# Logits of blocks 1, 4 and 5 from three bfloat16 pieces of h, four chunks at a time in four column ranges of TensorE's array

## The chip, the cores and the metric

The kernel runs on one core of one Trainium2 chip. The metric is the device time of one execution, in microseconds. Engines are called as the profile calls them: PE is TensorE's matrix multiply, PEld its weight load, DVE is VectorE, ACT ScalarE, POOL GpSimd, SP the engine that issues most DMAs.

## The reference, cut to what matters

Attention with random features gives x (2304 tokens by 512). A gated layer turns x into h (2304 by 1536) and y = h @ w_out. A gate then gives each token eight logits, and a greedy assignment over all logits sorts the tokens to eight experts, each a two-layer network.

```python
xn = x / rms * rms_g
g = xn @ w_gate
silu = g * (1.0 / (1.0 + np.exp(-g)))
val = xn @ w_val
y = silu * val @ w_out              # h = silu * val
logits = y @ moe2_w_gate            # 2304 x 8
order = np.argsort(-logits.flatten())   # greedy: token to expert, at most 288 each
```

The order of the logits decides where a token goes, so they are computed to nearly full float32. The kernel takes them from h with the product w_out @ moe2_w_gate (1536 by 8), made beforehand, so that they need not wait for y.

## The kernel before, in words

Tokens are cut into five blocks j = 0 to 4, four of 512 tokens and a last one of 256 (the title counts them from 1). The 1536 columns of h are cut into twelve chunks f of 128. One step (j, f, v) is twelve matmuls in `ffn_pe` (L659, L660, L662) into one of two PSUM buffers `gv`: v = 0 is the gate, v = 1 the value. After v = 0, ACT takes a tanh into `th` (L671) and DVE multiplies it in (L672); after v = 1, DVE makes the chunk of h (L684). ACT and POOL then split it into a high and a low part in `hp` (L686, L687), both of type float32r, and SP stores them to `h_dr` in DRAM, from where the later product with w_out reads them.

The logits of a chunk are two matmuls (`ffn_lg`, L698 and L699), with the chunk's 128 by 16 gate weights `wog` (a high and a low part for eight experts) as stationary operand and `hp`'s high and low part as moving operand, 512 or 256 columns wide. They stand in the step (j, f+1, 1), one chunk late, and sum over the twelve chunks in the PSUM tile `lg` (`late` for block 0). After chunk 11 ACT copies the 16 by 512 sums out (L702); in the next step `ffn_rank` transposes them in pieces of 16 by 128 (L710), ACT copies half of the result (L712), DVE adds the halves (L713), and `ranks` (L97 to L101) orders each token's eight logits.

Steps of blocks 0 to 2 and the first of block 3 run among the attention's work. Block 0's logits can't be done there, as `wog` is not ready: its h is stored unsplit. What is left then runs in a loop (L905 on): the rest of block 3, then block 4, and beside them block 0 "late": `late_load` (L891) fetches a chunk of block 0 from `h_dr` into a buffer `ht`, `late_split` (L897) splits it on ACT (L899) and POOL (L900) and stores it back, and `ffn_lg` takes its logits a step later. `wo_split` (ACT L876, DVE L877) prepares w_out, through staging buffers `ws`. In this loop Tile's scheduler orders the engines by priority; ahead of it PE's order is as written.

After the loop come six matmuls of y, the last chunk's logits (L1001), block 4's ranks, and `route`, the greedy assignment: a chain of small DVE operations and matmuls, with the product y = h @ w_out (`py`, L972, 648 matmuls of 512 columns) as filler on PE, in an order written by hand (`FILL`). `route` first clears two work areas on POOL (L122), one of them `ge6`.

Of the kernel before, what the change touches and what calls it, by code (L numbers as in the profile page):

```python
# [9 lines left out]
F32 = mybir.dt.float32  # L10
F32R = mybir.dt.float32r
BF = mybir.dt.bfloat16
I32 = mybir.dt.int32
AF = mybir.ActivationFunctionType
OP = mybir.AluOpType
AX = mybir.AxisListType
# [28 lines left out]
DW = 3  # L45
# [8 lines left out]
AHEAD_F = 150  # L54
HB = 6
LATE = 2

C_ID, C_SL, C_SA, C_C, C_P, C_E, C_T, C_N = 0, 128, 224, 248, 266, 267, 275, 339

# [44 lines left out]
def route(nc, keep, sb, ps, cst, L, R, ids, slot, aside, room):  # L104
# [10 lines left out]
    for n in (NSL, SL, 2 * NSL):  # L115
# [1 line left out]
        off += NC * n  # L117
    oa, ob, rt = parts
    ges = {5: room[:, off:off + (NC - 1) * 31 + 128],
           6: sb.tile([128, (NC - 1) * 63 + 128], BF, name="ge6", bufs=1)}  # L120
    for g in ges.values():
        nc.gpsimd.memset(g, 0.0)  # L122
    rt = rt.rearrange("p c (a n) -> p c a n", a=2)
# [168 lines left out]
def kernel(ctx, tc, qT, kT, kC, v1, vC, om, wgv, rms, wo, woT, wg2, w1, w2, cfd, trd, cid, out, dbg=None):  # L292
# [356 lines left out]


    fq, fst, lgs, rks = [], {}, [], []

    def ffn_pe(j, f, v):
        n = WIDTH[j]
# [10 lines left out]
    def ffn_el(j, f, v, pg):  # L665
        n = WIDTH[j]
        nh = n // HB2
        if v == 0:
            fst["th"] = fp.tile([128, BLK], F32, name="th")
            th = fst["th"][:, :n]  # L670
            nc.scalar.activation(th, pg, AF.Tanh, scale=0.5)  # L671
            nc.vector.scalar_tensor_tensor(th, th, 1.0, pg, op0=OP.add, op1=OP.mult)  # L672
            return
        th = fst["th"][:, :n]
        hp = fp.tile([128, BLK // HB2, 2, HB2], F32R, name="hp")
        hf = hp.bitcast(F32)
        dst = h_dr[nh * j:nh * j + nh] if nh > 1 else h_dr[NT // HB2 - 1:]
        dst = dst[:, :, f].rearrange("b p x -> p b x")
        if j == 0:
            nc.vector.scalar_tensor_tensor(hf[:, :, 0], pg.rearrange("p (b t) -> p b t", b=nh), 0.5,  # L680
                                           th.rearrange("p (b t) -> p b t", b=nh), op0=OP.mult, op1=OP.mult)
            nc.sync.dma_start(dst[:, :, :HB2], hf[:, :, 0])
            return
        nc.vector.scalar_tensor_tensor(th, pg, 0.5, th, op0=OP.mult, op1=OP.mult)  # L684
        h = th.rearrange("p (b t) -> p b t", b=nh)
        nc.scalar.copy(hp[:, :nh, 0], h)  # L686
        nc.gpsimd.tensor_sub(hp[:, :nh, 1], h, hp[:, :nh, 0])  # L687
        nc.sync.dma_start(dst, hf[:, :nh].rearrange("p b l t -> p b (l t)"))
        fq.append((j, f, hp))

    def ffn_lg(j, f, hp):
        n = WIDTH[j]
        nh = n // HB2
        if f == 0:
            st["lg", j] = (psL if j else psB).tile([2 * E, BLK], F32, name="lg" if j else "late", bufs=1)
        wv = wog[:, f].rearrange("p a e -> p (a e)")
        lg = st["lg", j][:, :n].rearrange("p (b t) -> p b t", b=nh)
        nc.tensor.matmul(lg, wv, hp[:, :nh, 0], start=(f == 0), stop=False)  # L698
        nc.tensor.matmul(lg, wv, hp[:, :nh, 1], start=False, stop=(f == KF - 1))  # L699
        if f == KF - 1:  # L700
            ls = fp.tile([2 * E, BLK], F32, name="th")
            nc.scalar.copy(ls[:, :n], st.pop(("lg", j))[:, :n])  # L702
            lgs.append((j, ls))

    def ffn_rank():
        for j, ls in lgs:
            n, c = WIDTH[j] // 128, j * BLK // 128
            pl = st["rank"]()
            for i in range(n):
                nc.tensor.transpose(pl[:, i, :], ls[:, i * 128:(i + 1) * 128], ident[:2 * E, :2 * E])  # L710
            lt = fp.tile([128, BLK // 128, E], F32, name="lt")
            nc.scalar.copy(lt[:, :n], pl[:, :n, E:])  # L712
            nc.vector.tensor_add(L[:, c:c + n, :], pl[:, :n, :E], lt[:, :n])  # L713
            rks.extend(range(c, c + n, 2))
        lgs.clear()

    st["eng"] = nc.gpsimd
    st["rank"] = lambda: psL.tile([128, BLK // 128, 2 * E], F32, name="lg")
# [6 lines left out]
    def ffn_step_pe():  # L725
        if not ready or ready[0][1:] not in gvs or (fq and fq[0][1] not in wogs):
            return False
        j, f, v = ready.pop(0)
        pg = ffn_pe(j, f, v)
        if (f, v) == (KF - 1, 1):  # L730
            del xblk[j]
        ffn_rank()
        if v and fq:
            ffn_lg(*fq.pop(0))
        fst["el"] = (j, f, v, pg)
        return True

    def ffn_step_el():
        if "el" in fst:
            j, f, v, pg = fst.pop("el")  # L740
            with tc.high_priority(offset=AHEAD_F):
                ffn_el(j, f, v, pg)
            ffn_rank_el()
            return j, f, v
        return None
# [96 lines left out]
    with tc.manual_schedule(engines={mybir.EngineType.PE}):  # L842
# [13 lines left out]
    rp = fc.enter_context(tc.tile_pool(name="rp", bufs=2))  # L856
    psB = fc.enter_context(tc.tile_pool(name="psB", bufs=2, space=PSUM))
    st["eng"] = nc.vector
    st["rank"] = lambda: psB.tile([128, 512], F32, name="num", bufs=1)[:, :BLK // 128 * 2 * E].rearrange(
        "p (c e) -> p c e", e=2 * E)  # L860
    ci = rp.tile([128, cid.shape[1]], I32, name="ci", bufs=1)
    ones = rp.tile([128, 128], BF, name="ones", bufs=1)
    pw = {sh: rp.tile([128, 128], BF, name=f"pw{sh}", bufs=1) for sh in SHIFTS}
# [7 lines left out]
    def wo_split(c):  # L871
        sv = stage.tile([128, 2, DM], F32, name="ws")
        nc.sync.dma_start(sv, wo_dr[2 * c:2 * c + 2].rearrange("f p d -> p f d"))
        w = wpool.tile([128, 2, 1024], F32R, name="wc")
        sv = sv.rearrange("p f d -> p (f d)")
        nc.scalar.copy(w[:, 0], sv)  # L876
        nc.vector.tensor_sub(w[:, 1], sv, w[:, 0])  # L877
        wos.append(w)
# [7 lines left out]

    order = [*range(BLK // 128, NC - TAIL), *range(BLK // 128), *range(NC - TAIL, NC)]
    seq2 = [(c, g) for c in order for g in range(3)]
    lates, step = [], 0

    def late_load(f):  # L891
        hs = f2.tile([128, 4, 2, 128], F32R, name="ht", bufs=HB)
        hs = hs.rearrange("p a l t -> p (a l t)").rearrange("p (b l t) -> p b l t", b=BLK // HB2, l=2)
        nc.sync.dma_start(hs.bitcast(F32)[:, :, 1], h_dr[:BLK // HB2, :, f, :HB2].rearrange("b p x -> p b x"))
        lates.append(hs)

    def late_split(f):  # L897
        hs = lates[f]
        nc.scalar.copy(hs[:, :, 0], hs.bitcast(F32)[:, :, 1])  # L899
        nc.gpsimd.tensor_sub(hs[:, :, 1], hs.bitcast(F32)[:, :, 1], hs[:, :, 0])  # L900
        nc.sync.dma_start(h_dr[:BLK // HB2, :, f].rearrange("b p x -> p b x"),
                          hs.bitcast(F32).rearrange("p b l t -> p b (l t)"))

    late_load(0)
    while True:  # L905
        if not ffn_step_pe():
            break
        lf, lv = divmod(step, 2)
        if not lv and 0 < lf <= KF:
            ffn_lg(0, lf - 1, lates[lf - 1])  # L910
        j, f, v = ffn_step_el()
        if lv and lf < KF:
            late_split(lf)
            if lf + 1 < KF:
                late_load(lf + 1)
        if j == NB - 1 and v:
            if f % 2 and f > 1:
                wo_split((f - 3) // 2)
            if f > 6:
                ffn2_load(*seq2[f - 7])  # L920
        step += 1
    assert step > 2 * KF
    wo_split(KF // 2 - 1)

    wch = {}
# [72 lines left out]
        return True  # L998

    fill(3 * FILL_MM)  # L1000
    ffn_lg(*fq.pop(0))  # L1001
    fill(3 * FILL_MM)
    ffn_rank()
    ffn_rank_el()
# [213 lines left out]
```

## Time and profile before

| | us |
|---|---|
| median of three runs | 923.66 (919.81 to 926.49) |
| the profiled execution | 922.03 |
| its span, first to last instruction | 920.2 |
| PE busy | 901.9 (98% of the span) |
| PEld busy | 783.3 |
| DVE busy | 554.2 (60%) |
| ACT busy | 372.8 |
| POOL busy | 229.8 |

The span is from the first to the last instruction; the profiled execution's own time holds 1.8 us more. Matmuls are pipelined, so a busy PE is not a PE at its peak: what a matmul costs is read from the distance of two starts, not from its duration.

### The profile page before, as it was taken

How to read it: one execution, taken by the hardware profiler on the slowest of the kernel's cores; microseconds unless marked ns; L12 is line 12 of the kernel's file. 1: busy time of each engine (PE TensorE's matmuls, PEld its weight loads, DVE VectorE, ACT ScalarE, POOL GpSimd, SP SyncE). 2: the span in 40 equal slices, each digit the busy share in tenths (PEclk: the TensorE clock that was granted, in tenths of full speed). 3: DMA queues.
4: the chain of work that ended last, by engine and by line, in shares of the span. 5: the costliest groups of instructions: out<-in, count | busy, mean ns of one | idle time of the engine just before them, and what ended most of it. 6: DMA issues, size and time to landing. Idle time of an engine off the chain costs nothing.

```text
span 920.2 us, 16173 instructions
## 1 busy us (share of the span) xinstructions
PE 901.9 (98%) x6171; PEld 783.3 (85%) x6171; DVE 554.2 (60%) x1262; ACT 372.8 (41%) x843; POOL 229.8 (25%) x298
## 2 busy tenths in 40 slices
PE   8998999999999999999999999999999999999996
PEld 7887888888888888877799777777779999999995
DVE  4798896565676775332273666666654655556661
ACT  5985565435554445333252001000014454544541
POOL 1355352122233332275232000000012222122111
PEclk9999999999999999999999999999999999999998
DMA  8556354444345552187564776776623666665550
GB/s 295 182 160 213 120 168 127 135 152 144 115 153 178 184 185 90 69 278 277 189 225 152 202 207 191 211 206 201 171 78 115 193 188 193 189 208 193 184 161 26
DMA packets 113213, 158.88 MB, mean 173 GB/s; under 512 B 6640, under 2 KB 70768, under 8 KB 113136
## 3 DMA queue, kind: packets, MB, share of 16 engines
q1 hardware_dynamic: 107328, 143.57, 49.4%
q0 software_dynamic: 3072, 9.44, 3.4%
q10 hardware_dynamic: 2736, 4.85, 1.4%
q8 instruction: 48, 0.79, 0.3%
q14 instruction: 29, 0.24, 0.1%
HBM read 113.79 MB, written 44.04 MB: 172 GB/s over the span
## 4 chain that ended last, share of the span: by engine, by line
PE 84%; issue 7%; DVE 5%; POOL 2%; DMA 2%; ACT 1%; SPq 0%; POOLq 0%; ACTq 0%; DVEq 0%
PE py L972 16%; PE gv L659 10%; PE gv L660 10%; PE gv L662 10%; PE pm L497 3%; PE ph L1086 3%; PE ph L1083 3%; PE ph L1084 3%; PE py L1094 3%; PE py L1095 3%; PE py L1096 3%; PE pm L440 2%; PE cnt L181 2%; PE pm L486 2%; PE pp L388 1%
## 5 line engine op out<-in xcount | busy, mean ns | idle before, releaser
L659 PE MATMUL gv<-xh,wc 128*128 128x512 f32 (+1 forms) x480 | 180.9, 383 | 2.5 <-DVE th L672 1.9
L660 PE MATMUL gv<-xh,wc 128*128 128x512 f32 (+1 forms) x480 | 175.3, 372 | 0.0
L972 PE MATMUL py<-wc,ht 128*128 128x512 f32 x648 | 167.1, 404 | 0.0
L972 PEld LDWEIGHTS py<-wc,ht 128*128 128x128 f32 x648 | 114.9, 189 | 19.0
L662 PE MATMUL gv<-xl,wc 128*128 128x512 f32 (+1 forms) x480 | 118.4, 369 | 0.0
L659 PEld LDWEIGHTS gv<-xh,wc 128*128 128x128 f32 x480 | 91.1, 190 | 19.5 <-DVE th L672 3.0
L660 PEld LDWEIGHTS gv<-xh,wc 128*128 128x128 f32 x480 | 91.2, 190 | 13.9
L662 PEld LDWEIGHTS gv<-xl,wc 128*128 128x128 f32 x480 | 85.5, 189 | 15.9
L400 ACT ACTIVATE ft<-pp,mx 128x128 f32<-128x128 f32 x288 | 82.3, 372 | 18.5 <-DVE mx L397 16.0
L687 POOL TENSOR_TENSOR hp<-th,hp 128x512 fp32r<-128x512 f32 (+1 forms) x48 | 60.6, 1262 | 114.5 <-ACT hp L686 102.6
L672 DVE SCALAR_TENSOR_TENSOR th<-th,gv 128x512 f32<-128x512 f32 (+1 forms) x60 | 37.9, 632 | 84.4 <-ACT th L671 84.4
L943 DVE TENSOR_TENSOR wc<-ws,wc 128x512 fp32r<-128x512 f32 x128 | 84.8, 683 | 0.0
L1094 PE MATMUL py<-ehh,wc 128*128 128x288 f32 x256 | 77.7, 304 | 0.0
L1095 PE MATMUL py<-ehl,wc 128*128 128x288 f32 x256 | 75.9, 297 | 0.0
L1096 PE MATMUL py<-ehh,wc 128*128 128x288 f32 x256 | 75.8, 296 | 0.0
L1083 PE MATMUL ph<-exh,wc 128*128 128x288 f32 x256 | 71.6, 302 | 0.0
L1084 PE MATMUL ph<-exh,wc 128*128 128x288 f32 x256 | 69.8, 295 | 0.0
L983 ACT COPY ys<-py 128x512 f32<-128x512 f32 x18 | 10.6, 587 | 144.6 <-PE py L972 103.7
L953 ACT CAST wc<-ws 128x1024 fp32r<-128x1024 f32 x64 | 66.9, 1046 | 2.7 <-ACT ys L983 2.4
L397 DVE TENSOR_REDUCE mx<-pp 128x4 f32<-128x512 f32 (+1 forms) x76 | 50.0, 657 | 16.6 <-PE pp L393 10.1
L1088 DVE SCALAR_TENSOR_TENSOR ehl<-ph,ehh 128x288 fp32r<-128x288 f32 x64 | 29.3, 458 | 46.8 <-ACT ehh L1087 46.8
L671 ACT ACTIVATE th<-gv 128x512 f32<-128x512 f32 (+1 forms) x60 | 33.2, 554 | 59.4 <-PE gv L662 52.0
(214 smaller groups left out, 1717.5 us busy)
## 6 DMA issues: line engine op xcount, KB each, us to landing
ws<-in_w_dram SPq DMA_DIRECT2D x64, 512.0 KB, 4.3
ht<-h_dr SPq DMA_DIRECT2D x54, 512.0 KB, 4.1
h_dr<-hp SPq DMA_DIRECT2D x36, 512.0 KB, 2.9
ws<-in_wgv_dram SPq DMA_DIRECT2D x24, 512.0 KB, 4.3
h_dr<-hp SPq DMA_DIRECT2D x24, 256.0 KB, 2.3
ws<-in_woT_dram SPq DMA_DIRECT2D x12, 512.0 KB, 3.6
ws<-in_wo_dram SPq DMA_DIRECT2D x12, 512.0 KB, 3.7
h_dr<-ht SPq DMA_DIRECT2D x12, 512.0 KB, 3.1
```

Of the source, the lines that this page charges most:

```text
L400: nc.scalar.activation(ft[:n, g], pp[:n, g], AF.Exp, bias=mx[:n, g:g + 1])
L659: nc.tensor.matmul(pg[:, :n], w[:, 0, v, k], xh[:, k, :n], start=(k == 0), stop=False)
L660: nc.tensor.matmul(pg[:, :n], w[:, 1, v, k], xh[:, k, :n], start=False, stop=False)
L662: nc.tensor.matmul(pg[:, :n], w[:, 0, v, k], xl[:, k, :n], start=False, stop=(k == KD - 1))
L943: nc.vector.tensor_sub(w[:, 1, h], sv[:, h], w[:, 0, h])
L953: nc.scalar.copy(w[:, 0], sv)
L972: nc.tensor.matmul(py, ht[:, i4, a], w[:, l, f % 2], start=(f == 0 and n == 0), stop=(f == KF - 1 and n == 2))
L1083: nc.tensor.matmul(ph, w[:, 0, k, m], xh[:, k], start=(k == 0), stop=False)
L1084: nc.tensor.matmul(ph, w[:, 1, k, m], xh[:, k], start=False, stop=False)
L1094: nc.tensor.matmul(py, w[:, 0, k], hh[:, k], start=(k == 0), stop=False)
L1095: nc.tensor.matmul(py, w[:, 0, k], hl[:, k], start=False, stop=False)
L1096: nc.tensor.matmul(py, w[:, 1, k], hh[:, k], start=False, stop=(k == KE - 1))
```

## The change

For blocks 3 and 4 and the late block 0 the logits are taken in another way. Each chunk of h in float32 is cut into three bfloat16 pieces: the upper half word of h, the upper half word of the rest, and what is left (`split3`, two subtractions on DVE; the third piece is written into the lower half word of h). The gate's weights are cut once into three bfloat16 pieces, which with eight columns of zeros make 32 stationary columns (`wb`). `group` takes four chunks: three rounds of four matmuls, each round one piece, each of the four chunks with its own 32 of the array's 128 columns and its own 32 partitions of the PSUM tile. All partial sums lie in 128 partitions; they are transposed in pieces of 128 by 128, and one DVE reduction adds the 16 partial sums of each logit.

The loop becomes `tail`, with PE's order as written: a group follows the matmuls of a step as soon as four chunks were born two or more steps before. The pieces of blocks 0, 3 and 4 lie in buffers `ht`, `ws` and `xl`. `late_load` is called for three chunks ahead of the loop; `late_split` still splits on ACT and POOL for the store, now into two `dw` buffers stored by two DMAs. One chunk of block 3 that is waiting when the loop starts is put together again from `hp` and cut. `ge6` is shared by `wb` and `route`. The matmuls of the steps, ACT's and POOL's splits of h and their stores stay.

```diff
@@ ffn_el
-        nc.vector.scalar_tensor_tensor(th, pg, 0.5, th, op0=OP.mult, op1=OP.mult)
-        h = th.rearrange("p (b t) -> p b t", b=nh)
+        pc = st["pieces"](j, f) if "pieces" in st else None
+        hs = pc[:, 0] if pc is not None else th
+        nc.vector.scalar_tensor_tensor(hs, pg, 0.5, th, op0=OP.mult, op1=OP.mult)
+        h = hs.rearrange("p (b t) -> p b t", b=nh)
...
-        fq.append((j, f, hp))
+        if pc is None:
+            fq.append((j, f, hp))
+        else:
+            split3(pc)
+            pq.append((j, f, pc))
+
+    def half(t, i):
+        return t.bitcast(BF).rearrange("p (t w) -> p t w", w=2)[:, :, i]
+
+    def split3(pc):
+        h, r = pc[:, 0], pc[:, 1]
+        nc.vector.tensor_sub(r, h, half(h, 1))
+        nc.vector.tensor_sub(half(h, 0), r, half(r, 1))
+
+    def group(four):
+        for n in range(3):
+            for i, (j, f, pc) in enumerate(four):
+                if ("lg", j) not in st:
+                    st["lg", j] = (psL if j else psB).tile([128, BLK], F32, name="lg" if j else "late", bufs=1)
+                src = (half(pc[:, 0], 1), half(pc[:, 1], 1), half(pc[:, 0], 0))[n]
+                nc.tensor.matmul(st["lg", j][32 * i:32 * i + 32, :WIDTH[j]], st["wb"][:, f], src,
+                                 start=(j, i) not in begun, stop=n == 2, skip_group_check=True)
+                begun.add((j, i))
+        for j, f, _ in four:
+            if f == KF - 1:
+                ls = fp.tile([128, BLK], F32, name="th")
+                nc.scalar.copy(ls[:, :WIDTH[j]], st.pop(("lg", j))[:, :WIDTH[j]])
+                wide.append((j, ls))
@@ ffn_rank
+        for j, ls in wide:
+            n, c = WIDTH[j] // 128, j * BLK // 128
+            pl = st["rank"]()
+            for i in range(n):
+                nc.tensor.transpose(pl[:, i, :], ls[:, i * 128:(i + 1) * 128], ident)
+            nc.vector.tensor_reduce(out=L[:, c:c + n, :], in_=pl[:, :n].rearrange("p c (g e) -> p c e g", e=E),
+                                    axis=AX.X, op=OP.add)
+            rks.extend(range(c, c + n, 2))
+        wide.clear()
@@ the loop
+    st["rank"] = lambda: psB.tile([128, 512], F32, name="num", bufs=1).rearrange("p (c e) -> p c e", e=128)
...
+    def tail():
+        for j, f, hp in fq:
+            pc = pieces(j, f)
+            nc.vector.tensor_add(pc[:, 0].rearrange("p (b t) -> p b t", t=HB2), hp[:, :, 0], hp[:, :, 1])
+            split3(pc)
+            pq.append((j, f, pc))
+        fq.clear()
+        step, born, gone, turns, nsplit = 0, [], 0, 0, 0
+        while ffn_step_pe():
+            if step > 1 and born[step - 2] - gone >= 4:
+                four = [pq.pop(0) for _ in range(4)]
+                group(four[turns:] + four[:turns])
+                gone, turns = gone + 4, (turns + 1) % 4
+            j, f, v = ffn_step_el()
+            if nsplit < KF and (step % 2 == 0 or step == 1):
+                late_split(nsplit)
+                nsplit += 1
+            elif step % 2 and len(lates) < KF:
+                late_load(len(lates))
...
     def late_split(f):
-        hs = lates[f]
-        nc.scalar.copy(hs[:, :, 0], hs.bitcast(F32)[:, :, 1])
-        nc.gpsimd.tensor_sub(hs[:, :, 1], hs.bitcast(F32)[:, :, 1], hs[:, :, 0])
+        pc = lates[f]
+        hi, lo = (fp.tile([128, DM], F32, name="dw", bufs=DW) for _ in range(2))
+        nc.scalar.copy(hi.bitcast(F32R), pc[:, 0])
+        nc.gpsimd.tensor_sub(lo.bitcast(F32R), pc[:, 0], hi.bitcast(F32R))
+        for n, w in enumerate((hi, lo)):
+            nc.sync.dma_start(h_dr[:BLK // HB2, :, f, n * HB2:(n + 1) * HB2].rearrange("b p x -> p b x"),
+                              w.rearrange("p (b x) -> p b x", x=HB2))
+        split3(pc)
+        pq.append((0, f, pc))
...
     fill(3 * FILL_MM)
-    ffn_lg(*fq.pop(0))
+    group(pq)
     fill(3 * FILL_MM)
```

## Rows read from the trace of the kernel before

**Rows 1.** The page's list of engines: busy us (share of the span), instructions.
```profile
span 920.2 us, 16173 instructions
PE 901.9 (98%) x6171; PEld 783.3 (85%) x6171; DVE 554.2 (60%) x1262; ACT 372.8 (41%) x843; POOL 229.8 (25%) x298
```

**Rows 2.** Busy time by stretch: loop with block 3, with block 4, then `route`.
```profile
core 0: us, PE busy (x) PEld busy (x) DVE busy (x) ACT busy (x) POOL busy (x), PEclk, DMA share, GB/s
397.00:460.60 63.60, 63.60 (x281) 48.68 (x280) 15.30 (x25) 18.15 (x31) 28.97 (x26) 1.00 0.71 248
460.60:500.40 39.80, 39.80 (x326) 37.82 (x325) 21.98 (x52) 16.49 (x34) 14.18 (x14) 1.00 0.62 208
502.00:660.00 158.00, 157.86 (x1389) 118.49 (x1389) 104.95 (x363) 15.63 (x23) 0.09 (x1) 1.00 0.69 198
```

**Rows 3.** PE's timeline at two pairs of 512-wide logit matmuls: start, duration, instruction.
```profile
402.42 0.39 PE L698 MATMUL lg<-hp,wog 128*16 128x512 f32 x1
...
403.34 0.39 PE L659 MATMUL gv<-xh,wc 128*128 128x512 f32 x1
```

**Rows 4.** PE's timeline at one pair of 256-wide logit matmuls.
```profile
471.97 0.28 PE L698 MATMUL lg<-hp,wog 128*16 128x256 f32 x1
472.09 0.28 PE L699 MATMUL lg<-hp,wog 128*16 128x256 f32 x1
472.21 0.29 PE L659 MATMUL gv<-xh,wc 128*128 128x256 f32 x1
```

**Rows 5.** PE's and PEld's timelines about the transposes of 16 rows.
```profile
465.43 0.64 PE L662 MATMUL gv<-xl,wc 128*128 128x256 f32 x4
466.00 0.42 PE L710 MATMUL num<-cf,th 16*128 16x16 f32 x4
466.35 0.39 PE L659 MATMUL gv<-xh,wc 128*128 128x256 f32 x1
466.57 0.28 PE L660 MATMUL gv<-xh,wc 128*128 128x256 f32 x1
465.31 0.55 PEld L662 LDWEIGHTS gv<-xl,wc 128*128 128x128 f32 x4
```

**Rows 6.** Groups by line and form: count, busy us and mean ns, idle before.
```profile
L687 POOL TENSOR_TENSOR hp<-th,hp 128x512 fp32r<-128x512 f32 x36 | 47.5, 1319 | 88.8 <-ACT hp L686 76.9 <-issue 8.2 <-DVE wog L646 3.6
L672 DVE SCALAR_TENSOR_TENSOR th<-th,gv 128x512 f32<-128x512 f32 x48 | 32.9, 685 | 72.7 <-ACT th L671 72.6
L900 POOL TENSOR_TENSOR ht<-ht 128x512 fp32r<-128x512 f32 x12 | 15.5, 1300 | 9.3 <-ACT ht L899 9.3
L551 DVE TENSOR_TENSOR xl<-pm,xh 128x512 fp32r<-128x512 f32 x18 | 12.3, 684 | 1.7 <-ACT xh L550 1.4 <-PE gv L662 0.3
L877 DVE TENSOR_TENSOR wc<-ws,wc 128x1024 fp32r<-128x1024 f32 x6 | 7.3, 1221 | 1.6 <-ACT wc L876 1.6
L698 PEld LDWEIGHTS lg<-hp,wog 128*16 128x16 f32 x48 | 4.6, 95 | 1.6 <-ACT hp L686 0.2
```

**Rows 7.** DVE and POOL at once: the same DVE operation with POOL at work, and without.
```profile
395.17 1.37 POOL L900 TENSOR_TENSOR ht<-ht 128x512 fp32r<-128x512 f32 x1 [0.23 <-ACT ht L899]
395.31 1.38 DVE L98 TENSOR_TENSOR rk_q<-L 128x128 f32<-128x128 f32 x1
398.00 0.28 DVE L98 TENSOR_TENSOR rk_q<-L 128x128 f32<-128x128 f32 x1
```

**Rows 8.** The timelines of DVE, ACT and PE from the last step to the first count of `route`.
```profile
500.42 0.42 DVE L684 SCALAR_TENSOR_TENSOR th<-gv,th 128x256 f32<-128x256 f32 x1 [0.54 <-PE gv L662]
502.47 0.36 ACT L702 COPY th<-lg 16x256 f32<-16x256 f32 x1 [1.19 <-PE lg L699]
503.59 0.17 DVE L713 TENSOR_TENSOR L<-num,lt 128x16 f32<-128x16 f32 x1 [2.75 <-ACT lt L712]
505.95 1.32 DVE L170 TENSOR_TENSOR ge<-s,ci 128x1116 bf16<-128x1116 f32 x1
```

**Rows 9.** One line's instructions: ns min/median/max, first and last start.
```profile
L122 POOL MEMSET ge<- x1: 1090/1090/1090, 393.8 to 393.8; 128x1199 bf16 x1
```

More of the change, by code (lines that the diff above doesn't have):

```diff
@@ L56 @@
 LATE = 2
+GE6 = (NC - 1) * 63 + 128
 C_ID, C_SL, C_SA, C_C, C_P, C_E, C_T, C_N = 0, 128, 224, 248, 266, 267, 275, 339
@@ L119, in route @@
     ges = {5: room[:, off:off + (NC - 1) * 31 + 128],
-           6: sb.tile([128, (NC - 1) * 63 + 128], BF, name="ge6", bufs=1)}
+           6: sb.tile([128, GE6], BF, name="ge6", bufs=1)}
     for g in ges.values():
@@ L651 @@
     fq, fst, lgs, rks = [], {}, [], []
+    pq, wide, begun = [], [], set()
     def ffn_pe(j, f, v):
@@ L709, in ffn_rank @@
             for i in range(n):
-                nc.tensor.transpose(pl[:, i, :], ls[:, i * 128:(i + 1) * 128], ident[:2 * E, :2 * E])
+                nc.tensor.transpose(pl[:, i, :2 * E], ls[:, i * 128:(i + 1) * 128], ident[:2 * E, :2 * E])
             lt = fp.tile([128, BLK // 128, E], F32, name="lt")
-            nc.scalar.copy(lt[:, :n], pl[:, :n, E:])
+            nc.scalar.copy(lt[:, :n], pl[:, :n, E:2 * E])
             nc.vector.tensor_add(L[:, c:c + n, :], pl[:, :n, :E], lt[:, :n])
@@ L858 @@
     st["eng"] = nc.vector
-    st["rank"] = lambda: psB.tile([128, 512], F32, name="num", bufs=1)[:, :BLK // 128 * 2 * E].rearrange(
-        "p (c e) -> p c e", e=2 * E)
+    st["rank"] = lambda: psB.tile([128, 512], F32, name="num", bufs=1).rearrange("p (c e) -> p c e", e=128)
     ci = rp.tile([128, cid.shape[1]], I32, name="ci", bufs=1)
@@ L888, with room4, pieces @@
     seq2 = [(c, g) for c in order for g in range(3)]
-    lates, step = [], 0
+    lates, grown = [], {}
+    def room4():
+        ht = f2.tile([128, 4, 2, 128], F32R, name="ht", bufs=HB)
+        return ht.bitcast(F32).rearrange("p f l t -> p (f l t)").rearrange("p (a t) -> p a t", a=2)
+    def pieces(j, f):
+        if WIDTH[j] == BLK:
+            return room4()
+        if f == 0:
+            grown[j] = xp.tile([128, KD, BLK], F32R, name="xl").bitcast(F32).rearrange(
+                "p k t -> p (k t)").rearrange("p (i a t) -> p i a t", i=4, a=2)
+        return grown[j][:, f % 4]
@@ new lines, in tail @@
+    def tail():
[17 more added lines that the diff above has]
+                late_load(len(lates))
+            if j == NB - 1 and v:
+                if f % 2 and f > 1:
+                    wo_split((f - 3) // 2)
+                if f > 6:
+                    ffn2_load(*seq2[f - 7])
+            born.append(gone + len(pq))
+            step += 1
+        assert step > 2 * KF and len(pq) == 4
@@ L891, in late_load @@
     def late_load(f):
[L892 to L895, printed above, removed]
+        pc = room4() if f % 3 == 2 else stage.tile([128, 2, BLK], F32, name="ws")
+        nc.sync.dma_start(pc[:, 0].rearrange("p (b x) -> p b x", x=HB2),
+                          h_dr[:BLK // HB2, :, f, :HB2].rearrange("b p x -> p b x"))
@@ L897, in late_split @@
+        lates.append(pc)
     def late_split(f):
-        hs = lates[f]
-        nc.scalar.copy(hs[:, :, 0], hs.bitcast(F32)[:, :, 1])
-        nc.gpsimd.tensor_sub(hs[:, :, 1], hs.bitcast(F32)[:, :, 1], hs[:, :, 0])
[L901 to L921, printed above, removed]
@@ L922 @@
-    assert step > 2 * KF
+        pc = lates[f]
[7 more added lines that the diff above has]
+        pq.append((0, f, pc))
@@ new lines @@
+    wb = rp.tile([128, GE6], BF, name="ge6", bufs=1)[:, :KF * 32].rearrange("p (f e) -> p f e", e=32)
+    wt = room4().rearrange("p a t -> p (a t)")[:, :KF * 2 * E].rearrange("p (f a e) -> p f a e", a=2, e=E)
+    st["wb"] = wb
+    nc.vector.memset(wb, 0.0)
+    nc.vector.tensor_add(wt[:, :, 0], wog[:, :, 0], wog[:, :, 1])
+    nc.vector.tensor_copy(wb[:, :, :E], wt[:, :, 0])
+    nc.vector.tensor_sub(wt[:, :, 1], wt[:, :, 0], wb[:, :, :E])
+    nc.vector.tensor_copy(wb[:, :, E:2 * E], wt[:, :, 1])
@@ L923 @@
+    nc.vector.tensor_sub(wb[:, :, 2 * E:3 * E], wt[:, :, 1], wb[:, :, E:2 * E])
+    for f in range(3):
+        late_load(f)
+    st["pieces"] = pieces
+    with tc.manual_schedule(engines={mybir.EngineType.PE}):
+        tail()
     wo_split(KF // 2 - 1)
```

## The prediction

> **What bounds the kernel now.** I read the page's list of engines first: PE is busy for 901.9 of 920.2 us, DVE for 60% [rows 1]. A share over the whole span proves nothing for one stage, so the busy times by stretch come next. In the loop, from 397.0 to 500.4, PE has no idle time in either part; in `route`, from 502 to 660, it lacks 0.14 us of 158 [rows 2]. The granted clock is 1.00, the upper level of 2.4 GHz, throughout. So PE sets the end here, and a microsecond less of PE work in the loop is a microsecond less of time, as long as nothing else makes PE wait. The reader should see two more things in these rows. DVE has 15.3 of 63.6 us to do in block 3's part and 22.0 of 39.8 in block 4's: room, but not without end. And POOL has 29.0 in block 3's part. The third view is PE's own timeline, for the true price of a logit matmul; the fourth the groups by form, for what DVE and POOL pay; the fifth DVE and POOL side by side.
>
> **What is removed.** Twelve pairs for each of three blocks. Four 512-wide logit matmuls start at 402.42 and the next step at 403.34 [rows 3]: 0.23 us each. Blocks 0 and 3 have 48: 11.0 us. A 256-wide pair takes 0.24 us, from 471.97 to 472.21 [rows 4], so block 4's 24 cost 2.9. Together 13.9 us of PE, all in stretches where PE is the bound.
>
> **What is added on PE.** 36 chunks are nine groups, six of 512 and three of 256 columns, each three rounds of four matmuls. No row shows matmuls in separate column ranges. If a round's four run at once, a group costs three matmuls: 6 x 3 x 0.23 + 3 x 3 x 0.12 = 5.2 us. If they run one after another, 72 x 0.23 + 36 x 0.12 = 20.9. I take 5.2, since the four share no column and no output partition, and keep both. The price is taken as the same for bfloat16 read from every other half word as for float32r; no row separates them.
>
> A group cuts the array in another way than the steps around it. The nearest row is the transposes with 16 rows, the only ones here that use a part of the array's rows: four 256-wide matmuls start at 465.43, so they have streamed by 465.91; the next step's second matmul starts at 466.57 where, without the transposes, 466.03 would do [rows 5]. That is 0.54 us for four tiny transposes. At some 0.06 each (an estimate, half of what a 256-wide matmul takes) 0.3 are left, 0.15 for each of two changes. Eighteen changes make 2.7 us; bounds are nothing and 0.27 each, 4.9.
>
> Weight loads: a load of 16 columns lasts 95 ns [rows 6], and loads lie under the streaming of the matmul ahead (four from 465.31 to 465.86, under matmuls from 465.43 [rows 5]), so I take nothing for 108 of them; uncovered they cost 108 x 0.095 = 10.3.
> The Trainium skill speaks against me here: TensorE: Matmul & The Clock Gate, section Part 3: Packing small matmuls — row/col tiling, says that a weight load overlaps matmuls in flight only when its row group differs, and column ranges share all rows. The trace does not follow it for the whole array [rows 5]; for column ranges no run here shows it yet. The same section gives 3.07 times for four packed matmuls, by which 5.2 would be an estimated 6.8.
>
> The transposes become whole ones: ten instead of ten, without the change of the array's cut that [rows 5] hold. I count zero; bounds are a gain of 1.3 (three sets' 0.54, with the ten at the same 0.06) and a loss of 1.
>
> So the work of PE falls by 13.9 - 5.2 - 2.7 = 6.0 us.
>
> **What is added on DVE, and what waits for it.** Each 512-wide chunk has two subtractions more, at 0.684 like L551's [rows 6]: 1.37 us, and 24 chunks make 33; a 256-wide one costs 2 x 0.42 (as L684's short form [rows 8]), and twelve make 10. In steady state two steps of block 3 take PE 24 x 0.23 = 5.5 us plus half a group, 0.5: 6.0. In them DVE has two L672/L684 at 0.685 and two splits: 4.1. That fits. But both operands of these subtractions lie in SBUF, and there the same DVE operation took 1.38 us instead of 0.28 while POOL's L900 ran [rows 7]: it started and then stood until POOL ended. In two steps POOL has one L687 and one L900, 1.32 + 1.30 = 2.6 us [rows 6]. If all of that fell on DVE, DVE would need 6.7 of 6.0. L672 stands behind these subtractions in DVE's queue; it frees the `gv` buffer that the step after next needs, and so PE waits for it. Below 6.0 the buffers take it up: I count 0.8 for the whole rest of the loop, with 0 and ten times 0.7 as bounds.
>
> The first group comes soonest: behind the fourth step, 4 x 12 x 0.23 = 11.0 us into the loop. Before it DVE must do four L672/L684 (2.7), put one chunk together (0.7), split four (5.5) and prepare the weights, some five operations near 0.28 [rows 7] (1.4): 10.3. POOL has three L900 and two L687 then, 6.5. Half of it on DVE gives 13.6, 2.6 late; as part may start ahead of the loop, I take 2.0, with 0 and 5.8 as bounds.
>
> One wait is sure. Blocks 0 and 3 end in one group, so `ffn_rank` transposes both in a row into the single `num` buffer, and PE's order is now as written: block two's transposes, and every step behind them, wait until DVE has reduced block one's 512 elements. That takes 0.7 (L551's form), or 1.9 if an L877 of 1.22 stands ahead [rows 6]; I take 1.2. In block 4 the same step of DVE's queue is tight, since two steps take PE 3.0 us and DVE 1.7, or 2.9 with an L877; this is in the 0.8.
>
> **What costs nothing.** ACT and POOL do the same splits as before. The second store of each late chunk goes through SP, ahead of which no compute waits except by `dw` buffers; if these ran out, ACT's tanh would stand behind L899's successor and this would be part of the port's stall. The clear of `ge6`, 1.09 us [rows 9], moves behind the last group but has until L170 at 505.95 [rows 8], on an idle POOL (0.09 busy in 158 us [rows 2]); without that cover it costs 1.1. Block 4's end: L684 is done at 500.84 and L713 starts at 503.59 [rows 8]; two subtractions, a group, the copy and a reduction of 0.42, without ACT's second copy, give the same within 0.3, under y's matmuls.
>
> **The sum.** -6.0 + 2.0 + 1.2 + 0.8 = -2.0 us. The profiled execution of 922.03 (its span and 1.8 around it) becomes 920.0; it lies 1.6 below the median, so the median of 923.66 becomes 921.7.
>
> **The rivals.**
> *No waits* (0.25): DVE keeps up, as 4.1 in 6.0 says. Then -6.0, 917.7; with free changes of the cut -8.7, 915.0. Against it speak [rows 7].
> *DVE and POOL in each other's way* (0.18), on the other side: the subtractions stand behind POOL in every pair of steps. Ten pairs at 0.7 are 7.0, with 2.0 and 1.2 that is 10.2 - 6.0 = +4.2, 927.9. It decides from the point where these waits together pass 6.0, that is, when more than 1.9 of POOL's 2.6 us in a pair fall on DVE. For it: [rows 7]; against it: L672 and L684 read one operand from PSUM, and POOL may yield as often as DVE.
> *The ranges don't run at once* (0.08): the change doesn't do what it says. 20.9 + 2.7 - 13.9 = +9.7, plus the rank's 1.2 (longer groups give DVE its time back): 934.6.
> *Weight loads uncovered* (0.07): -6.0 + 10.3 + 1.2 = +5.5, 929.2. This is what the section of the Trainium skill named above would do here.
>
> **How the numbers follow.** The forecast holds 0.42, its own range being -5 to +1, 918.7 to 924.7. The range of 915.0 to 930.0 takes in no waits with free changes below and both middling losses above; it leaves out the serial ranges (0.08) and the tails of the port case and of the gains (0.12). About 1%, 9.2 us, is what a measurement can tell from no change. Faster than 914.4 needs every cost at its lower bound and more: 0.03. Slower than 932.9 needs serial ranges or both kinds of stall at their upper bounds: 0.10. Within: 0.87.
>
> **What would show it.** Right: a 512-wide group with starts of one round within 0.1 us and about 1.0 us between the steps around it; a PE gap ahead of the first group, and one between two sets of four transposes. Wrong: 0.23 between all twelve starts (serial), a loop free of gaps (no waits), or PE waiting for L672 in most steps (port).

## The result and the profile after

The changed kernel takes 932.39 us (median of four, 930.92 to 935.08) against 923.44 for the kernel before. The ratio is 1.0102, with a 95% interval of 1.0058 to 1.0146. It is about 1% slower, with the interval clear of no change, and outside the range of the prediction (915.0 to 930.0). The profiled execution took 932.95 us with a span of 931.2.

The page's list of engines, and busy time by the same three stretches as in [rows 1, 2], in the same columns:

```profile
span 931.2 us, 16386 instructions
PE 903.4 (97%) x6207; PEld 781.0 (84%) x6207; DVE 608.1 (65%) x1341; ACT 372.7 (40%) x840; POOL 231.7 (25%) x298
...
397.00:460.60 63.60, 57.40 (x280) 42.78 (x280) 47.61 (x61) 15.44 (x26) 27.02 (x23) 0.97 0.55 187
460.60:500.40 39.80, 38.26 (x289) 33.49 (x291) 32.03 (x68) 15.42 (x28) 13.17 (x14) 1.00 0.85 278
502.00:660.00 158.00, 155.61 (x1343) 117.55 (x1342) 104.27 (x357) 17.24 (x27) 3.76 (x5) 0.99 0.65 190
```

In [rows 2] PE was busy for all of the first two stretches. Now it lacks 6.2 us of 63.6 and 1.5 of 39.8, and DVE is busy for 47.6 us where it had 15.3 (this holds the time for which an instruction has started and stands). PE's own waits from 384 to 520 us (what it waited for, total us, times, longest):

```profile
PE gv L662 <- DVE th L675: 7.5, 8, 3.4
PE cnt L183 <- DVE ge L172: 2.4, 1, 2.4
PE num L752 <- DVE L L753: 0.2, 1, 0.2
```

Together 10.1 us; in the kernel before the same window holds one wait of 0.2, for POOL. L675 is the L672 of the kernel before: it frees the `gv` buffer for the step after next. L172 (before: L170) is the first comparison of `route`.

What PE was to gain is there. PE's timeline at a 512-wide group and the steps around it, beside [rows 3]:

```profile
418.65 1.07 PE L665 MATMUL gv<-xl,wc 128*128 128x512 f32 x4
419.65 0.40 PE L714 MATMUL late<-ht,ge 128*32 128x512 bf16 x1
419.65 0.40 PE L714 MATMUL lg<-ht,ge 128*32 128x512 bf16 x1
419.65 0.40 PE L714 MATMUL late<-ws,ge 128*32 128x512 bf16 x1
419.66 0.40 PE L714 MATMUL lg<-ht,ge 128*32 128x512 bf16 x1
419.88 0.39 PE L714 MATMUL late<-ht,ge 128*32 128x512 bf16 x1
...
420.49 0.50 PE L662 MATMUL gv<-xh,wc 128*128 128x512 f32 x1
420.82 0.40 PE L663 MATMUL gv<-xh,wc 128*128 128x512 f32 x1
```

The weight loads of this group (PEld's timeline), and of all groups (count, busy us and mean ns, idle before):

```profile
419.64 0.38 PEld L714 LDWEIGHTS <-ge 128*32 128x32 bf16 x12 [0.35 <-issue]
...
L714 PEld LDWEIGHTS <-ge 128*32 128x32 bf16 x108 | 2.5, 94 | 4.8 <-issue 3.5
```

Four column ranges start within 0.01 us, and the next round 0.23 later. From 416.83 to 418.65 eight 512-wide matmuls start 0.2275 us apart, so the four of L665 have streamed by 418.65 + 4 x 0.2275 = 419.56; without a group the next step's second matmul would stand at 419.79, and it stands at 420.82. So a group costs 1.03 us: three rounds of 0.23 and 0.34 for the two changes of the array's cut. Its 108 weight loads of 94 ns would be 10.2 us one after another; they cover 2.5.

### The profile page after: what moved, and what is told of

Same layout as the page of the kernel before. It is cut to its first block, busy times and chain, and to the rows that moved or that the text cites. A ratio compares the mean times of both kernels' runs of the same rounds, so it can differ in the third digit from the quotient of the medians.

```text
span 931.2 us, 16386 instructions
## 1 busy us (share of the span) xinstructions
PE 903.4 (97%) x6207; PEld 781.0 (84%) x6207; DVE 608.1 (65%) x1341; ACT 372.7 (40%) x840; POOL 231.7 (25%) x298
## 4 chain that ended last, share of the span: by engine, by line
PE 74%; issue 9%; DVE 8%; POOL 4%; DMA 3%; ACT 1%; SPq 0%; POOLq 0%; ACTq 0%; DVEq 0%
PE py L1052 15%; PE gv L662 8%; PE gv L663 8%; PE gv L665 7%; PE pm L499 3%; PE ph L1166 3%; PE ph L1163 3%; PE ph L1164 3%; PE py L1174 3%; PE py L1175 3%; PE py L1176 3%; PE pm L442 2%; PE cnt L183 2%; PE pm L488 2%; PE pp L390 1%
## 5 line engine op out<-in xcount | busy, mean ns | idle before, releaser
L662 PE MATMUL gv<-xh,wc 128*128 128x512 f32 (+1 forms) x480 | 183.5, 389 | 10.1 <-DVE th L675 9.6
L1052 PE MATMUL py<-wc,ht 128*128 128x512 f32 x648 | 170.0, 407 | 0.0
L665 PE MATMUL gv<-xl,wc 128*128 128x512 f32 (+1 forms) x480 | 118.7, 369 | 0.0
L665 PEld LDWEIGHTS gv<-xl,wc 128*128 128x128 f32 x480 | 85.9, 190 | 16.0
L675 DVE SCALAR_TENSOR_TENSOR th<-th,gv 128x512 f32<-128x512 f32 (+1 forms) x60 | 37.7, 629 | 32.1 <-ACT th L674 32.0
L573 ACT ACTIVATE dw<-ws 128x512 f32<-128x512 f32 x48 | 32.3, 678 | 46.2 <-DMA ws<-in_wo_dram 18.2
```

Source lines behind the costliest of these rows:

```text
L662: nc.tensor.matmul(pg[:, :n], w[:, 0, v, k], xh[:, k, :n], start=(k == 0), stop=False)
L665: nc.tensor.matmul(pg[:, :n], w[:, 0, v, k], xl[:, k, :n], start=False, stop=(k == KD - 1))
L1052: nc.tensor.matmul(py, ht[:, i4, a], w[:, l, f % 2], start=(f == 0 and n == 0), stop=(f == KF - 1 and n == 2))
```

## Where PE's wait comes from

DVE, POOL and PE ahead of the first group, from their timelines (start, duration, instruction, and for PE the idle time before it):

```profile
400.48 1.74 POOL L692 TENSOR_TENSOR hp<-ht,hp 128x512 fp32r<-128x512 f32 x1
...
400.99 1.38 DVE L99 TENSOR_TENSOR rk_g<-L 128x128 f32<-128x128 f32 x1
402.29 0.28 DVE L100 TENSOR_TENSOR rk_q<-L 128x128 f32<-128x128 f32 x1
402.49 1.58 DVE L706 TENSOR_TENSOR ht<-ht 128x512 bf16<-128x512 f32 x2
...
405.20 0.68 DVE L675 SCALAR_TENSOR_TENSOR th<-th,gv 128x512 f32<-128x512 f32 x1
...
405.93 0.50 PE L662 MATMUL gv<-xh,wc 128*128 128x512 f32 x1 [3.40 <-DVE th L675]
```

L99 takes 1.38 us here, where the same form took 0.28 at 397.71: it stands until about the end of POOL's L692, 402.2. This is the pattern of [rows 7]. Behind it come the subtractions, and only behind those L675, for which PE waits 3.40 us. The groups of DVE and of POOL from 396 to 516 us (busy us, mean ns, then idle before):

```profile
L706 DVE TENSOR_TENSOR ht<-ht 128x512 bf16<-128x512 f32 x16 | 16.4, 1031 | 8.6 <-POOL hp L692 8.5
L705 DVE TENSOR_TENSOR ht<-ht 128x512 f32<-128x512 f32 x15 | 14.4, 962 | 0.3
L706 DVE TENSOR_TENSOR xl<-xl 128x256 bf16<-128x256 f32 x12 | 5.5, 462 | 7.2 <-POOL hp L692 7.1
...
L692 POOL TENSOR_TENSOR hp<-ht,hp 128x512 fp32r<-128x512 f32 x11 | 16.1, 1459 | 24.6 <-ACT hp L691 24.6
```

The 512-wide subtractions last 0.96 and 1.03 us on average, not the 0.684 of [rows 6], and POOL's L692 lasts 1.46 where its counterpart L687 took 1.32. The second one, L706, also waits for a semaphore of POOL's L692: it overwrites the lower half word of the h that L692 is still reading. The prediction had not seen that wait.

So three theories stood after this reading. **W**: the wait of L706 for POOL. **P**: subtractions of DVE and POOL exclude each other, whoever yields. **D**: DVE simply has too much to do.

## The experiments

Each ratio is to runs of the kernel before that were taken together with that experiment; all were 922.6 to 923.1 in the median.

**e1: the wait of L706 removed.** The third piece goes into the lower half word of the rest, which POOL does not read.

```diff
-        nc.vector.tensor_sub(half(h, 0), r, half(r, 1))
+        nc.vector.tensor_sub(half(r, 0), r, half(r, 1))
```

> One thing is undone: the third piece is written into the lower half word of the rest r, no longer into that of h, and the third round reads it there. The arithmetic is the same. POOL's split of h (L692, L981) still reads h, but nothing writes h after it any more, so the second subtraction (L706) has no reason to wait for POOL. Theory W (the second subtraction stood behind POOL's read of h, 19 times, 18.4 us of DVE standing still, and L675 behind it made PE wait): L706's idle time falls from 18.4 us to under 2, PE's waits for L675 (7.5 us with its own list of the loop) fall to under 2, and the time falls to 918 to 924. Theory P (the two engines hold each other up at SBUF, which made L705 and L706 take up to 1.8 us in place of 0.69): the subtractions stay stretched and the time stays at 929 to 933. Theory D (DVE simply has too much work): 927 to 932.

931.58 us, 1.0095 (1.007 to 1.012): no change. DVE's and POOL's groups, then PE's waits:

```profile
L706 DVE TENSOR_TENSOR ht<-ht 128x512 bf16<-128x512 f32 x16 | 19.1, 1194 | 0.4
L705 DVE TENSOR_TENSOR ht<-ht 128x512 f32<-128x512 f32 x16 | 17.0, 1062 | 0.3
...
L692 POOL TENSOR_TENSOR hp<-ht,hp 128x512 fp32r<-128x512 f32 x11 | 19.4, 1763 | 21.6 <-ACT hp L691 21.6
```

```profile
PE gv L662 <- DVE th L675: 7.8, 8, 2.7
PE cnt L183 <- DVE ge L172: 2.2, 1, 2.2
```

The waits ahead of L706 are gone (0.4 instead of 8.5 us for this form), and the time is the same. The two 512-wide forms have grown from 30.8 to 36.1 us instead, and POOL's L692 from 1.46 to 1.76 us on average. W alone falls: with the semaphore or without it, L675 comes as late. Between P and D this run does not decide, as both expected this time.

**e2: e1, with POOL reading nothing.** POOL's subtractions for blocks 0, 3 and 4 become memsets of the same size, which leaves out the low part of h there.

```diff
-        nc.gpsimd.tensor_sub(hp[:, :nh, 1], h, hp[:, :nh, 0])
+        nc.gpsimd.memset(hf[:, :nh, 1], 0.0)
...
-        nc.gpsimd.tensor_sub(lo.bitcast(F32R), pc[:, 0], hi.bitcast(F32R))
+        nc.gpsimd.memset(lo, 0.0)
```

> As e1, and besides the low part of h is left out for blocks 0, 3 and 4: POOL clears it (a memset that reads nothing) in place of subtracting, so y is less exact for these blocks. POOL then reads no SBUF beside DVE. Theory W: within 3 us of e1, since the wait was the matter. Theory P: only here do L705 and L706 fall to 0.69 us (512 wide) throughout, and the time falls by 5 or more below e1, to 917 to 922. Theory D: no different from e1.

923.22 us, 1.0003 (0.9986 to 1.002): 8.4 us less than e1, with DVE's instructions the same in number and size. The fall is over the 5 us expected; the time is 1.2 us above the range of 917 to 922. DVE's groups, then PE's waits, then POOL and DVE side by side:

```profile
L709 DVE TENSOR_TENSOR ht<-ht 128x512 bf16<-128x512 f32 x15 | 11.4, 758 | 0.4
L708 DVE TENSOR_TENSOR ht<-ht 128x512 f32<-128x512 f32 x15 | 10.3, 686 | 0.3
```

```profile
PE cnt L183 <- DVE ge L172: 2.2, 1, 2.2
PE gv L662 <- DVE th L675: 2.1, 2, 1.3
```

```profile
398.40 0.53 POOL L695 MEMSET hp<- 128x512 f32 x1
398.86 0.53 POOL L984 MEMSET dw<- 128x512 f32 x1
...
398.70 0.68 DVE L708 TENSOR_TENSOR ht<-ht 128x512 f32<-128x512 f32 x1
```

The subtractions last 0.686 and 0.758 us now, and PE's waits for L675 fall to 2.1. P stands; D as the whole cause falls. A memset is also shorter than a subtraction, 0.53 us, but that is not what frees DVE: the subtraction at 398.70 lies wholly under two memsets and takes 0.68.

**e3: the groups alone.** No subtractions on DVE: all three rounds read the first piece, so the logits here are those of a truncated h.

```diff
-        nc.vector.tensor_sub(r, h, half(h, 1))
-        nc.vector.tensor_sub(half(h, 0), r, half(r, 1))
+        pass
...
-                src = (half(pc[:, 0], 1), half(pc[:, 1], 1), half(pc[:, 0], 0))[n]
+                src = half(pc[:, 0], 1)
```

> As the changed kernel without the two subtractions of split3: all three rounds of a group read the upper half word of h, so the logits are those of a bfloat16 h. It shows what the groups alone bring. By the distances in the trace after, a 512-wide group costs 1.02 us and a 256-wide one 0.65, together some 8.4 against 13.9 removed: 5.5 less. All theories: 916 to 920, with PE's waits for L675 in the loop under 1 us; if it stays above 924, neither DVE nor POOL is the cause but PE's order or the transposes.

918.49 us, 0.9947 (0.9927 to 0.9967). PE's only wait:

```profile
PE gv L662 <- DVE th L675: 1.6, 1, 1.6
```

It is longer than the 1 us expected, and there is none in `route`. PE's part of the change, its order as written included, is a gain.

**e4: ACT makes both parts of h.** Nothing is left out: the high part is ACT's copy of the upper half word, the low part ACT's copy of the rest that DVE makes anyway. POOL's subtractions go.

```diff
     def split3(pc, hi=None, lo=None):
         h, r = pc[:, 0], pc[:, 1]
+        if hi is not None:
+            nc.scalar.copy(hi, half(h, 1).rearrange("p (b t) -> p b t", t=HB2))
         nc.vector.tensor_sub(r, h, half(h, 1))
+        if lo is not None:
+            nc.scalar.copy(lo, r.rearrange("p (b t) -> p b t", t=HB2))
         nc.vector.tensor_sub(half(h, 0), r, half(r, 1))
```

> The changed kernel, with POOL's two subtractions per pair of steps (for h's low part, blocks 0, 3 and 4) gone without leaving work out: the high part is ACT's copy of the upper half word of h, the low part ACT's copy of the rest that DVE makes anyway. DVE's instructions stay the same in number and size; ACT has 3.1 us in a pair of steps of 6.0 (tanh 0.60 and four copies at 0.62). P (DVE's and POOL's subtractions hold each other up): the subtractions fall from 0.95 and 1.03 us to 0.69 and 0.75, PE's waits for L675 from 7.5 us to under 2.5, the time to 920 to 924. D (DVE simply has too much to do, 4.1 of 6.0 plus the rest): waits and time stay, 930 or more. A third way, ACT late: PE waits for L675 which waits for ACT's tanh, over 5 us, 928 or more.

920.07 us, 0.997 (0.9952 to 0.9988): by the ratios some 12 us less than the changed kernel, and below the kernel before. DVE's groups, then PE's waits:

```profile
L710 DVE TENSOR_TENSOR ht<-ht 128x512 bf16<-128x512 f32 x16 | 12.2, 765 | 0.4
L707 DVE TENSOR_TENSOR ht<-ht 128x512 f32<-128x512 f32 x16 | 11.0, 690 | 0.3
```

```profile
PE cnt L183 <- DVE ge L172: 2.2, 1, 2.2
PE gv L662 <- DVE th L675: 0.8, 1, 0.8
```

The same subtractions take 0.690 and 0.765 us with no subtraction of POOL's beside them; of 7.5 us of waits for L675, 0.8 remain. ACT makes four copies in a pair of steps instead of two, and no wait of PE shows it. e4 is 3 us under e2, with intervals that just overlap; where that comes from was not followed.

**e5: the changed kernel with block 4's logits as before**, to see whether the wait in `route` comes from block 4's end.

```diff
-        pc = st["pieces"](j, f) if "pieces" in st else None
+        pc = st["pieces"](j, f) if "pieces" in st and j < NB - 1 else None
```

> The changed kernel, but block 4's logits made as in the kernel before (two float32r matmuls of 16 columns a chunk, no third piece, no subtractions of DVE for it); the groups remain for blocks 0 and 3. If the 2.4 us for which PE waits in route, with its clock at 0.70 to 0.87 behind it, come from the longer chain at block 4's end and from y matmuls used up between block 4's steps: that wait goes, -2.4 and some -1.4 of the clock's, PE gets 24 x 0.12 - 3 x 0.65 = 0.9 more, and the time falls by about 3, to 929.5; the waits for L675 in block 3's part stay at 5 to 7.5 us. If the end's wait is only a delay carried over from block 3's part, it stays at over 1.5 us and the time is 932 to 934.

929.33 us, 1.0072 (1.0046 to 1.0098). The wait in `route` falls from 2.4 to 0.3 us, the waits for L675 stay at 7.0. Two waits for block 4's `hp` come in, 2.0 us together. The median falls by the 3 us expected, but the intervals of the two kernels overlap, and the edit also takes 24 subtractions from DVE.

**e6: work put into the gap of 3.40 us.** Fourteen matmuls whose sums nobody reads, ahead of the fourth step.

```diff
+            if step == 3:
+                for _ in range(14):
+                    nc.tensor.matmul(junk, wsl[0][:, 0, :128], xblk[NB - 2][0][:, 0], start=True, stop=True)
```

> The changed kernel with 14 matmuls of 512 columns, whose sums nobody reads, in PE's queue ahead of the fourth step of the loop, where PE stood for 3.40 us: 14 x 0.23 = 3.2 us of work in a gap that is there anyway. If the gap is what made the granted clock fall (0.66 in 406 to 411), the clock stays at 1.00, the step behind it takes 2.8 us instead of 4.5, and the time is 1 to 2 us less, 930.5 to 931.5. If the clock falls for another reason, 0.66 stays and the time is the same, 932 to 933. PE's total wait for L675 falls by about 3 in either case, which by itself gives nothing back.

933.0 us, 1.0101 (1.0069 to 1.0133). The granted clock from 406 to 411 is 1.00 (0.66 in the changed kernel), as expected; the time is not less. A gap of 1.01 us had opened two steps earlier, so the fourteen ran from 404.44 to 407.77 and pushed the step back by 1.8 us; the first group starts at 410.70 instead of 410.46. On the time it is inconclusive.

**e7: e4 and e5 together.**

```diff
-        pc = st["pieces"](j, f) if "pieces" in st else None
+        pc = st["pieces"](j, f) if "pieces" in st and j < NB - 1 else None
```

> Both: ACT makes both parts of h for blocks 0 and 3, so that POOL subtracts nothing there, and block 4's logits are made as in the kernel before. P and the end's chain together: waits for L675 under 2.5 us, no wait in route, PE's work 13.9 - 2.9 - 6 x 1.03 = 4.8 us less than in the kernel before; 918 to 921, below the kernel before. If the loss has another cause, 926 or more.

920.88 us, 0.9971 (0.9955 to 0.9987): the same as e4. The wait in `route` is 0.3 instead of 2.2, and nothing is gained: block 4's logits cost PE more the old way, and PE waits 0.7 us for POOL's low part there.

**e8 and e9: e4 and e7 with PE's order at the end by hand.** In e4 the compiler's scheduler had moved 7 of y's matmuls between block 4's steps and 5 into the last group, which then runs in four pieces; for `route`'s first comparison too few were left.

```diff
-    fill(3 * FILL_MM)
-    group(pq)
-    fill(3 * FILL_MM)
-    ffn_rank()
-    ffn_rank_el()
+    with tc.manual_schedule(engines={mybir.EngineType.PE}):
+        fill(3 * FILL_MM)
+        group(pq)
+        fill(3 * FILL_MM)
+        ffn_rank()
+        ffn_rank_el()
```

> e4_act_makes_both_parts with the order of PE around the last group written by hand too, so that the matmuls of y stay where they are written: none between block 4's steps, none inside the last group, 21 behind the transposes, under the wait for the first comparison of route. In e4, 7 of them stand in the loop and 5 inside the last group, whose 12 matmuls take four changes of the cut more, and PE then waits 2.17 us for that comparison, with the granted clock at 0.86 in 500 to 512. If that wait and the split group are a loss of their own: the wait goes, some 2 to 3 us come back, 917 to 918.5, about what the groups alone gave (918.5). If PE's early matmuls of y only trade places with the wait: 919.5 to 921, and new gaps stand in the loop where the matmuls of y were.

> e7_act_and_block4_old with the same order by hand. It had no wait in route beyond 0.3 us and 4 matmuls of y in the loop; PE has 24 x 0.12 - 3 x 0.65 = 0.9 us more in block 4 than with groups, and two waits for POOL's h low part of 0.7 together. If the end's wait is a loss of its own, the order by hand gives less here than with the groups: 919 to 921, over e8 by 1 to 2.

e8: 918.25 us, 0.9956 (0.9937 to 0.9974), in the range expected. e9: 920.82, 0.9988 (0.9971 to 1.0005), 2.6 over e8 where 1 to 2 were expected: the order by hand gives nothing where the wait in `route` was already short. The end of e8 on PE:

```profile
499.38 0.38 PE L756 MATMUL num<-cf,th 128*128 128x128 f32 x2
499.51 5.02 PE L1054 MATMUL py<-wc,ht 128*128 128x512 f32 x21
504.38 0.61 PE L183 MATMUL cnt<-oh,ge 128*128 128x8 bf16 x18
```

21 matmuls of y stand behind the transposes and the first count follows without a wait, at 504.38 (507.72 in the kernel before). e8 is the fastest kernel of this study that leaves nothing out, 4.7 us under the kernel before and level with the groups alone. Against e4 it is 1.8 us less by the medians, with intervals that overlap.

**e10: the changed kernel with that order alone.** The edit is the one shown for e8.

> The changed kernel with POOL's subtractions left as they are, and only the order of PE around the last group written by hand (the edit that took e4 from 920.1 to 918.3). If the end's wait is a loss of its own, independent of the subtractions: it goes (2.4 us and the fall of the clock behind it), the waits for L675 stay at 6 us and more, and the time is 929 to 930.5. If DVE is so late in block 4's part that the comparison of route comes late whatever PE has left to do, or PE waits in the loop in its place: 931.5 to 933.

931.04 us, 1.0092 (1.0076 to 1.0109): as the changed kernel, and between the two ranges expected. PE's waits decide:

```profile
PE gv L662 <- DVE th L675: 9.9, 10, 3.0
PE lg L714 <- DVE xl L706: 1.0, 1, 1.0
```

PE's gap at the fourth step, and the window of one microsecond behind it (granted clock third from the end):

```profile
409.07 0.50 PE L662 MATMUL gv<-xh,wc 128*128 128x512 f32 x1 [3.03 <-DVE th L675]
```

```profile
409.00:410.00 1.00, 0.93 (x4) 0.80 (x5) 0.86 (x3) 0.16 (x1) 0.00 (x0) 1.00 0.00 0
```

The wait in `route` is gone, and in its place PE waits 9.9 us in the loop for L675 and 1.0 for L706. So the wait at the end is not a loss of its own here: while DVE is late, taking it away only shows the lateness elsewhere.

## Why the prediction was wrong, point by point

Term by term, in us. The last column is what each took from the span, read from starts (the clock from windows, below). A gap takes more than the profile's wait: the wait is counted from the modelled end of the matmul ahead, 0.16 us after the next one could have started, and behind the gap the second matmul follows 0.10 late. The gap at 427.59 shows both:

```profile
425.15 1.07 PE L665 MATMUL gv<-xl,wc 128*128 128x512 f32 x4
427.59 0.50 PE L662 MATMUL gv<-xh,wc 128*128 128x512 f32 x1 [1.37 <-DVE th L675]
427.92 0.40 PE L663 MATMUL gv<-xh,wc 128*128 128x512 f32 x1
```

The four have streamed by 425.15 + 0.91 = 426.06, so the second matmul could stand at 426.29; it stands 1.63 later, for a wait of 1.37. The eight gaps before a step's matmul take 0.26 each in this way, the other two 0.1 to 0.2.

| term | predicted | wait in the profile | taken from the span |
|---|---|---|---|
| PE's work | -6.0 | | -5.8 |
| ahead of the first group | +2.0 | 3.4 | 3.7 |
| the rank | +1.2 | 0.2 | 0.3 |
| waits for L672 (now L675), rest of the loop | +0.8 | 4.1 | 5.9 |
| block 4's end and the first count | 0 | 2.4 | 2.6 |
| last group cut into four | none | | 1.0 |
| granted clock | none | | 3.4 |
| sum | -2.0 | 10.1 | 11.1 (span: 11.0) |

**PE's gain: right.** With 13.9 us removed, six groups at 1.03 and three at 0.65 make 8.1 where the prediction had 5.2 + 2.7 = 7.9. A change of the cut costs 0.17 us (0.15). The 0.65 is read as the 1.03 was: in block 4, L665 starts at 499.59 and the next step's second matmul stands at 500.84. The groups alone gave 4.4 us (e3), near 5.8 less the one wait of 1.6 that e3 shows.

**The ranges, the weight loads: right.** Neither rival happened. The twelve loads of a group lie within 0.38 us from 419.64, beside rounds that start at 419.65, 419.88 and 420.11, and all 108 cover 2.5 us. By the rule on weight loads in the Trainium skill's TensorE: Matmul & The Clock Gate, section Part 3: Packing small matmuls — row/col tiling, loads for four column ranges, which share all rows, would not overlap matmuls in flight. The measurement decides. The 3.07 that the prediction took from the same section stands there for packing by rows; here four column ranges share the 0.23 us of one matmul.

**The port: the step that failed.** The prediction took 0.8 us for the rest of the loop, from 0 to 7, on the ground that DVE needs 4.1 of 6.0 us in a pair of steps and that POOL may yield as often as DVE. That is no relief. If two engines' instructions exclude each other, their times add whoever yields, and the prediction's own figure for this was 6.7 of 6.0. In e1 both sides grew at once, DVE's subtractions to 1.06 and 1.19 us and POOL's to 1.76. In place of the 0.8 the rest of the loop has 4.1 us of waits for L675 and loses 5.9; the gap at the fourth step is longer for the same reason, and a fall of the clock, which had no term, stands behind it. These three make 5.9 + 3.7 + 1.7 = 11.3 us. The 2.4 at the first count are not among them, as e2 and e4 have 2.2 there. DVE need not be full for that: in e1 L675 itself waits 11.3 us for its tanh in sum, and elsewhere stands behind stretched subtractions when PE needs it. With POOL reading nothing 8.4 us go (e1 to e2), with POOL not subtracting some 12 (the changed kernel to e4, by 1.0102 and 0.997): so much the exclusion and what follows from it cost. Without it the change gains 3 us (e4), near the 2.0 of the forecast. DVE's work as such, from e3's 0.9947 to e4, is at most a few us; their intervals overlap.
In e2, with a POOL that only writes, the subtractions take 0.69 and 0.76 us; L675, with one operand in PSUM, takes 0.674 to 0.683 us in the changed kernel, e1, e4, e5, e7 and e8 alike.
The Trainium skill, SBUF — State Buffer, section SBUF: two separate sides, says that a DVE operation with two SBUF inputs and a GpSimd operation that reads SBUF take one pair of ports in turn, each for its whole instruction. The runs agree.

**The rival that came true, and its price.** *DVE and POOL in each other's way* had 0.18 and +4.2 us, from 10.2 us of waits. That the waits are 10.1 is luck: the rival had 7.0 in ten pairs of steps, 2.0 and 1.2, and the trace has 4.1, 3.4 and 0.2, with 2.4 at a place where the rival had nothing. The span grew by 11.0, not 4.2. The rest lies in the ends of the gaps (the last column above), in the last group, cut into four by y's matmuls (three more pairs of changes of the array's cut, 1.0), and in the granted clock behind two of the gaps:

```profile
406.00:408.00 2.00, 2.00 (x6) 1.58 (x7) 1.36 (x2) 0.62 (x1) 0.60 (x1) 0.59 0.00 0
408.00:410.00 2.00, 2.00 (x7) 1.59 (x6) 0.73 (x1) 0.00 (x0) 0.67 (x1) 0.56 0.22 83
...
520.00:522.00 2.00, 2.00 (x6) 1.56 (x5) 1.13 (x1) 0.42 (x1) 0.00 (x0) 0.50 0.00 0
```

These are windows of the changed kernel (the clock is third from the end): near 0.50, the lower level of 1.2 GHz, instead of 1.00. At 0.59 and 0.56 PE loses 2 x 0.41 + 2 x 0.44 = 1.7 us behind the first gap, and at 0.75, 0.50 and 0.90 as much from 518 to 524. What the clock costs in the end stays open: e6 kept it up and e10 had a gap of 3.03 us without a fall, and neither was faster, which fits a DVE that sets the pace there.

**The first group: half right.** 3.40 us instead of 2.0, inside the bounds of 0 and 5.8. But the gap stands ahead of the fourth step, for a `gv` buffer; the group behind that step found its pieces ready and did not wait. Ranks on DVE and POOL, which the prediction left out, are in the chain.

**The transposes: right, and the rank covered.** From the first of four transposes to the second matmul behind them it is 0.58 us (473.07 to 473.65), as before (466.00 to 466.57). The bound of 1.3 for them does not come out of its own figures: 3 x 0.54 - 10 x 0.06 is 1.0. The rank took 0.3 us instead of 1.2, because the scheduler put four matmuls of y, 0.9 us, between the two sets of transposes; they were missing later, under `route`'s first comparison.

**Block 4's end: wrong.** "The same within 0.3": from L689's start to the end of the comparison it is 7.92 us (509.54 to 517.46) against 6.85, with L706 waiting 0.87 for POOL in it; and 11 of the 27 matmuls of y that cover it had been moved into the loop. It is these moved matmuls that are missing there: 7 stand behind the last transposes in the changed kernel and 8 in e2 and e4, where DVE is not late and PE still waits 2.2 us; with 17 (e3) and 21 (e8, e10) it does not wait. In e10 PE's waits moved into the loop instead; in e8, with DVE free, the order by hand gives at most a small gain.

**What the prediction named as the sign of the port case**, PE waiting for L672 in most steps, is not quite what the trace shows: eight waits, a single one of 3.4 us and seven under 1.4. The buffers take up the rest until DVE has fallen behind far enough.

## What to carry to other kernels

Before work goes to an engine with spare time, ask what it shares: a DVE subtraction with both operands in SBUF and a POOL subtraction are to be added up as if they were one engine's, and set against the time of the stage (here 6.7 against 6.0). A gap in PE costs more than the profile's wait: here 10.1 us of waits went with some 17 lost in the span (11.0 more than before, and the 5.8 that PE saved), the rest in the ends of the gaps, a split group and the clock behind them. If a change gains on one engine and loses on a shared port, look for the third engine: with ACT making both parts of h, and y's order by hand, the same change gives 4.7 us instead of losing 9.

## What was not expected of the hardware

- Taking away a semaphore wait for POOL gave nothing as long as both engines read SBUF: e1 had none of the 15.6 us for which L706 waited on L692, longer subtractions on both engines, and the same time.
- Gaps of nearly the same length did not all lower the clock: 3.40 us (changed kernel) and 3.05 (e5, 0.69 in 406 to 411) did, and so did 2.39 at the first count of the changed kernel (0.50 in 520 to 522); 3.03 (e10) did not.
- Weight loads of four column ranges overlap one another and the matmuls in flight: twelve loads of a group, 94 ns each, cover 0.38 us at 419.64, and the group's rounds start at 419.65, 419.88 and 420.11.
